# Another order in the opening of attention, weight loads behind the third row gather, and another chain at the list table

## Chip, cores and metric

One core of a Trainium2 chip runs the whole kernel. The metric is device time in microseconds of one launch; lower is better. The time before is the median of three runs.

## What is computed

Causal attention with a bias from a running sum, then a mixture of experts with greedy assignment by capacity, then a second mixture with top-1 routing and a residual:

```python
# attention: B=4, H=8, S=576, D=64, all float32
cum = np.cumsum(np.maximum(s, 0), -1)
scores = q @ k.T / 8 + np.minimum(-(cum[..., :, None] - cum[..., None, :]), 0)   # causal
attn = exp(scores - max) / (sum + 1e-9);  x = (attn @ v) as (2304, 512)
# first mixture: 8 experts, each takes 288 rows; the pairs (row, expert) in order of falling
# logit x @ w_gate; a row goes to the first expert that has room
for e: out[mask] = relu(x[mask] @ w1[e]) @ w2[e]
# second mixture: rows with x @ w_skip > 0 get x + prob * relu(x @ w1[e]) @ w2[e], e = argmax
```

## The kernel before, in words

PE's float32 products are made of two parts, a rounded high part (fp32r) and the low rest, so each product is two or three passes, and each operand has to be split first: a rounding copy (ACT or POOL) and a subtraction (DVE or POOL).

**Attention** works on 32 heads in groups of two (`G`), in steps `k`, three per head. Each step issues a hand-written order (`ORDER`) of scores (S, lines 236 and 237), masking (M, 248), exponentials (X, 256), transposes (T, 272), splits of the transposed weights (H, 286, and L, 291), the product with V (AV, 300) and the output. For a group `g`, `load_a` brings the raw rows of K and Q through SP (`load_raw`, line 80) and a rounded copy of them through POOL's DMA queue (line 88) into one of three buffers `KQ`. `load_b` puts four small DMAs with the running sums into the buffer (74, 75), copies halves of it into `ka` and `qa` by DMA on SP (140, 141), makes the low parts by POOL subtractions (143, 144; a pair for each of the two heads), and loads V (146). `vsplit` splits V on POOL (92, 93). Scores need `ka` and `qa`; AV needs the split V. Group 0 is split by DVE and ACT in `first_group`; the second head's low part is `low1` (110, 111). V of group 0 is split in `vload2`. `raw` has two buffers, so a load of raw rows waits for the subtractions of two groups before. Setup work for the later stages is interleaved on POOL through `gen`, one piece a step from step 9 on.

Every engine runs its queue in order. The sequence on POOL in the opening of the kernel before is: V split of group 0, subtractions of group 1, three memsets (387 to 389) that fill the constant rows of the third `KQ` buffer, the load of group 2, V split of group 1, the load of group 3, the subtractions of group 2.

**The first mixture.** `routing` finds for one expert at a time, by a search over the bit patterns on DVE with counts on PE, the logit threshold, and from it the 288 rows. They become three lists of 96 row numbers: a one-hot table `oh` (729) of each row's place, times the row's number in two digits `rv` (726), summed by 18 matmuls (734); two DVE operations (738, 739) turn the two digits into the row number `tok`. POOL gathers the rows by indirect DMA (993), PE transposes them (1004), ACT and DVE split them (1008, 1009). Then follow the first product with w1 (1018, 96 matmuls in eight blocks), and the second with w2 (1043, 1049). Weights come in eight loads of 512 KB for each expert: six are split by ACT (985) and DVE (987), two are used as they are. For the first expert SP issues loads 0 to 3, and ACT issues loads 4 to 7 (951) once it has converted the fourth. All this is not written in order by hand: each operation is given to a planner (`Plan`) with an engine, a cost, what it reads and writes, and a priority, and the planner's simulated start times set the order of every engine's queue, for the first mixture and the first expert of the second in one plan. `KN["nd"]` = 16 dummy matmuls (1410) are added after the lists, at the lowest priority. The table `oh` shares its tile with the constant `io1` (854, POOL).

Of the kernel before, what the change touches and what calls it, by code (L numbers as in the profile page):

```python
# [56 lines left out]
def attention(tc, ctx, consts, gen, kqT, kq0, vL, s, wgb, xs, logits, ident):  # L57
# [25 lines left out]
    def load_a(g):  # L83
        if g not in loads:
            load_raw(g)
        qb, kb, raw = QB[g % NQB], KB[g % NQB], loads[g]
        for sl in ((slice(0, 1), slice(1, 2)) if g == 1 else (slice(0, G),)):
            nc.gpsimd.dma_start(KQ[g % NQB][64:128, :, sl], kqT[g][:, :, sl])
        loads[g] = raw, qb, kb
# [41 lines left out]
    def load_b(g, eng, dq):  # L131
        h0 = g * G
        raw, qb, kb = loads.pop(g)
        qa = work.tile([128, G, S], F32R, name="qa")
        ka = work.tile([128, G, S], F32R, name="ka")
        vraw = work.tile([128, G, NB, D], F32, name="vraw", bufs=3)
        vhl = work.tile([128, G, NB, 2, D], F32R, name="vhl", bufs=3)
        aux_rows(h0, qb, kb)
        for sl in ((slice(0, 1), slice(1, 2)) if g == 1 else (slice(0, G),)):
            dq.dma_start(ka[0:64, sl].bitcast(F32), kb[64:128, sl].bitcast(F32))  # L140
            dq.dma_start(qa[64:128, sl].bitcast(F32), qb[64:128, sl].bitcast(F32))
        for i in range(G):
            eng.tensor_tensor(qa[0:64, i], raw[64:128, 1, i], qb[64:128, i].bitcast(F32), op=OP.subtract)  # L143
            eng.tensor_tensor(ka[64:128, i], raw[64:128, 0, i], kb[64:128, i].bitcast(F32), op=OP.subtract)
            if i == 0:
                nc.sync.dma_start(vraw, vL[g])
        grp[g] = (qa, ka, qb, kb, vhl, vraw)
        return lambda: vsplit(vraw, vhl, eng)
# [33 lines left out]
    nc.gpsimd.tensor_copy(gate, QB[0][0:4, G - 1, 0:1].bitcast(F32))  # L182
    load_a(1)
# [193 lines left out]
    if True:  # L377
        for k in range(nsteps + 12 + SK):
# [3 lines left out]
            if u0 and u0[1] == 1 and u0[0] % G == 0 and u0[0] // G + 1 < NH // G:  # L382
                g = u0[0] // G + 1
                if g == 1:
                    vload2()
                    fin = load_b(g, nc.gpsimd, nc.sync)
                    nc.gpsimd.memset(QB[2][0:64].bitcast(F32), 1.0)
                    nc.gpsimd.memset(KB[2][0:64].bitcast(F32), 0.0)
                    nc.gpsimd.memset(KB[2][0:4].bitcast(F32), 1.0)
                    load_a(g + 1)  # L390
                else:
                    if g + 1 < NH // G:
                        load_a(g + 1)
                    fin = load_b(g, nc.gpsimd, nc.sync)
                fin()
            if k == FILL:
                low1()
                fill()
# [132 lines left out]
def routing_consts(tc, consts, T):  # L531
# [16 lines left out]
    def steps():  # L548
# [8 lines left out]
        for o in range(2):  # L557
            v = c["vals"][64 * o:64 * o + 64]
            nc.gpsimd.iota(v[:, 0:4 * B, 0].rearrange("p (b n) -> p b n", b=B), pattern=[[S // 64, B], [2, 4]],
                           base=1 + o, channel_multiplier=0, allow_small_or_imprecise_dtypes=True)  # L560
            nc.gpsimd.iota(v[:, 4 * B:, 0], pattern=[[2 * S // 64, B // 2]], base=S // 64 * o, channel_multiplier=0,
# [23 lines left out]
def routing(tc, pool, P, c, lw, ph, ei_all, tok, rt, rb, T):  # L585
# [5 lines left out]
    sl_pr = -1 if ph == 0 else 1  # L591

# [113 lines left out]
    if not last:  # L706
        dve(0.08, "eo", "pn", lambda: V.tensor_scalar(pn, eo, -3e38, None, op0=OP.mult))
        dve(0.21, "pn", "lw", lambda: V.tensor_tensor(lw, lw, pn[:, None, :].to_broadcast(BC), op=OP.add))
        dve(0.08, "eo", "opn", lambda: V.tensor_tensor(opn, opn, eo, op=OP.subtract))
    dve(0.11, "pb", "inc", lambda: V.tensor_tensor_scan(inc, rt[:, 128:128 + 2 * NT], c["zero40"], 1.0, op0=OP.add,  # L710
# [4 lines left out]
    if not last:  # L715
        dve(0.08, "q", "q1", lambda: V.scalar_tensor_tensor(q1, q, CAP + 0.5, q, op0=OP.is_le, op1=OP.mult))
        dve(0.08, "q1", "nd", lambda: V.scalar_tensor_tensor(nd, q1, 0.5, nd, op0=OP.is_ge, op1=OP.add))

    rv, g4, p_, bk, iv = (T[n] for n in "rv g4 p_ bk iv".split())
# [12 lines left out]
    def lists():  # L732
# [5 lines left out]
    dve(0.075, "ib", "iv", lambda: V.tensor_copy(iv, rt[:96, 256:262].rearrange("p (k v) -> p k v", v=2)), sl_pr)  # L738
    dve(0.075, "iv", f"tok{ph}", lambda: V.scalar_tensor_tensor(  # L739
        tok[:, 3 * ph:3 * ph + 3], iv[:, :, 0], 64.0, iv[:, :, 1], op0=OP.mult, op1=OP.add), sl_pr)  # L740


def routing_tiles(pool):
# [26 lines left out]
    t("iv", [96, 3, 2])  # L770
# [59 lines left out]
def moe(tc, ctx, setup, lw, xs, w1, w2, w9, v1, v2, out, ident):  # L830
# [3 lines left out]
    for _ in gen:  # L834
# [20 lines left out]
                   allow_small_or_imprecise_dtypes=True)  # L855
    for i in (6, 7):
# [73 lines left out]
    def dmas():  # L930
        while done["dma"] < min(done["route"] * NCH, 2 * E * NCH):
# [5 lines left out]
            if p < E:  # L937
# [7 lines left out]
                if 4 <= n < 8:  # L945
                    if n == 4:
                        def ld(p=p):
                            reg["g"] = nc.scalar.value_load(ei_all[0:1, p:p + 1], min_val=0, max_val=E - 1)
                        op("ACT", 0.1, f"ei{p} wh3b", "regg", ld)
                    op("ACT", 0.07, "regg", key,  # L950
                       lambda p=p, dst=dst, k=k, src=src: nc.scalar.dma_start(
                           dst, src[ds(reg["g"], 1), k % 4].rearrange("o p f -> (o p) f")), xfer=1.456, lat=0.65)
# [14 lines left out]
    def conv():  # L967
# [19 lines left out]
        op("DVE", 1.13, f"raw{i} wh{j}a wh{j}b", v, lambda: V.tensor_tensor(  # L987
# [416 lines left out]

    def route(p):
        routing(tc, pool, cur["P"], rc, lw, p, ei_all, tok, rt, rb, T)
        done["route"] += 1
        if p == 0:
            for _ in range(KN["nd"]):
                op("PE", 0.43, "ib", "", lambda: nc.tensor.matmul(YB[0], rc["onesb"], T["ge"][:, 0:512], start=True,  # L1410
# [6 lines left out]
    for k in range(4):  # L1417
        conv()
    for k in range(3):
        xtr(0, k)  # L1420
    for p in range(E):
# [204 lines left out]
```

## Time and profile before

| | |
|---|---|
| median of three runs | 723.19 us (722.15 to 724.77) |
| the profiled execution | 724.78 us |
| its span in the trace | 723.1 us |
| PE busy, share of the span | 667.0 us, 92% |
| DVE busy | 531.7 us, 74% |
| ACT busy | 402.3 us, 56% |
| POOL busy | 269.2 us, 37% |
| mean granted PE clock | 0.960 |

The rows of the next sections come from this execution. In a timeline a row is: start in us, length in us, engine, line, operation, output<-inputs and sizes, xcount, and in brackets how long the engine had been idle and what released it. A queue of an engine (SPq, ACTq) shows DMA issues. The granted clock is a share of 2.4 GHz: 1.00 is that, 0.50 is 1.2 GHz. Attention takes the first 230 us, the first routing until 251, the first mixture until about 475, the second mixture the rest.

### The profile page before, as it was taken

What the parts mean: (1) busy time and instruction counts of PE and PEld (TensorE: products, weight loads), DVE (VectorE), ACT (ScalarE), POOL (GpSimd) and SP (SyncE); (2) the same over time, 40 slices, a digit from 0 to 9 for tenths busy, and PEclk for the clock granted to TensorE, in tenths of its full rate; (3) what the DMA queues carried; (4) which work ended last, traced back from release to release, by engine and by line L of the source; (5) the groups of instructions that cost most, each with busy time, mean ns of one, the idle gap of its engine ahead of it and who ended that gap; (6) DMA issues with size and microseconds to landing.
All of it is one profiled execution on the core that took longest, in us unless ns stands there. A gap on an engine that the chain in (4) does not pass through costs nothing. (4 is left out here: it accounts for less than half of the span.)

```text
span 723.1 us, 14104 instructions
## 1 busy us (share of the span) xinstructions
PE 667.0 (92%) x4667; PEld 581.1 (80%) x4667; DVE 531.7 (74%) x1604; ACT 402.3 (56%) x910; POOL 269.2 (37%) x379
## 2 busy tenths in 40 slices
PE   4789999999996469999999999999999999999996
PEld 4678989989895349787989898989988787777775
DVE  7668888898886656888888878763459449499544
ACT  8768888888883121443425242454347248487533
POOL 4899769968720420111112050522111321141201
PEclk9989999999998559999999989999999999999998
DMA  7868797797612340644527080943069219499320
GB/s 163 198 150 198 186 231 164 202 212 169 175 36 75 114 157 12 244 146 175 202 103 274 30 302 11 370 153 107 12 247 390 79 62 327 160 347 332 147 81 23
DMA packets 35939, 122.25 MB, mean 169 GB/s; under 512 B 6480, under 2 KB 6480, under 8 KB 34064
## 3 DMA queue, kind: packets, MB, share of 16 engines
q1 hardware_dynamic: 28272, 94.87, 41.2%
q0 software_dynamic: 7008, 24.25, 12.4%
q10 hardware_dynamic: 576, 2.10, 0.9%
q8 instruction: 43, 0.70, 0.4%
q14 instruction: 40, 0.33, 0.2%
HBM read 101.12 MB, written 13.76 MB: 159 GB/s over the span
## 5 line engine op out<-in xcount | busy, mean ns | idle before, releaser
L987 DVE TENSOR_TENSOR wl<-raw,wh 128x1024 fp32r<-128x1024 f32 x112 | 134.4, 1216 | 23.0 <-ACT wh L985 19.7
L985 ACT CAST wh<-raw 128x1024 fp32r<-128x1024 f32 x112 | 114.7, 1048 | 35.7 <-DMA raw<-in_w_dram 23.7
L256 ACT ACTIVATE z<-z,sums 128x576 f32<-128x576 f32 (+2 forms) x144 | 84.7, 589 | 3.2 <-DVE sums L248 1.6
L248 DVE CUSTOM_DVE_ANT_0 z<-s,mask 128x576 f32<-128x576 f32 (+2 forms) x144 | 70.3, 513 | 13.0 <-PE s L237 12.4
L272 PE MATMUL pt<-ident,z 128*128 128x128 f32 (+1 forms) x464 | 77.3, 282 | 1.1 <-DVE ptl L291 0.6
L993 POOL DMA_INDIRECT xb<-xs,k_tok x24 | 30.8, 1284 | 120.6 <-DVE k_tok L739 38.1
L291 DVE TENSOR_TENSOR ptl<-pt,pth 128x512 fp32r<-128x512 f32 (+2 forms) x128 | 68.0, 551 | 7.4 <-ACT pth L286 7.1
L236 PE MATMUL s<-kq 128*128 128x288 f32 (+2 forms) x192 | 63.8, 344 | 9.6 <-ACT kq L114 8.8
L1049 PE MATMUL y<-hf,rb 128*128 128x288 f32 x256 | 70.5, 411 | 0.0
L1093 POOL DMA_INDIRECT out_dram<-xb,k_tok x24 | 26.2, 1091 | 114.3 <-ACT xb L1076 97.8
L286 ACT CAST pth<-pt 128x512 fp32r<-128x512 f32 (+2 forms) x128 | 59.1, 473 | 10.9 <-PE pt L272 8.1
L237 PE MATMUL s<-ka,qa 128*128 128x288 f32 (+2 forms) x192 | 52.5, 309 | 7.5 <-DMA qa<-kq 4.6
L272 PEld LDWEIGHTS pt<-ident,z 128*128 128x128 f32 (+1 forms) x464 | 52.8, 142 | 6.2 <-issue 3.0
L1051 ACT CAST yr<-y 128x288 fp32r<-128x288 f32 x32 | 12.7, 398 | 74.1 <-PE y L1049 70.8
L1049 PEld LDWEIGHTS y<-hf,rb 128*128 128x128 f32 x256 | 45.5, 190 | 9.0
L1018 PE MATMUL h<-xth,wh 128*128 128x288 f32 x256 | 50.5, 318 | 2.0 <-DVE r_ac L663 0.9
L300 PE MATMUL y<-pth,vhl 128*128 128x384 f32 (+2 forms) x160 | 50.8, 326 | 0.2 <-ACT yT L317 0.2
L1018 PE MATMUL h<-xtl,wh 128*128 128x288 f32 x256 | 48.4, 309 | 0.1
L1018 PE MATMUL h<-xth,wl 128*128 128x288 f32 x256 | 48.1, 306 | 0.0
L236 PEld LDWEIGHTS s<-kq 128*128 128x128 f32 x192 | 37.0, 193 | 13.4 <-issue 11.1
L300 PE MATMUL y<-ptl,vhl 128*128 128x384 f32 (+2 forms) x160 | 46.6, 320 | 0.0
L143 POOL TENSOR_TENSOR qa<-raw,kq 64x576 fp32r<-64x576 f32 x30 | 42.6, 1419 | 4.3 <-DVE ptl L291 2.5
(343 smaller groups left out, 1736.5 us busy)
## 6 DMA issues: line engine op xcount, KB each, us to landing
raw<-in_v_dram SPq DMA_DIRECT2D x64, 512.0 KB
raw<-in_w_dram SPq DMA_DIRECT2D x46, 512.0 KB
raw<-in_kqT_dram SPq DMA_DIRECT2D x14, 576.0 KB
kq<-in_kqT_dram POOLq DMA_DIRECT2D x14, 576.0 KB
rb<-in_w_dram SPq DMA_DIRECT2D x14, 512.0 KB
vraw<-in_vL_dram SPq DMA_DIRECT2D x16, 320.0 KB
xs<-xb SPq DMA_DIRECT2D x16, 288.0 KB
ka<-kq SPq DMA_DIRECT2D x14, 288.0 KB
```

What stands on the lines that cost most here:

```text
L236: nc.tensor.matmul(rows[:, o + c0:o + c1], qs_, kb[:, i, c0:c1], start=True, stop=False)
L237: nc.tensor.matmul(rows[:, o + c0:o + c1], ql_, ka[:, i, c0:c1], start=False, stop=True)
L248: nc.vector.tensor_tensor_reduce(z[:, :w], ps[:, o:o + w], mk, op0=OP.add, op1=OP.min, scale=-0.125, scalar=3e38, accum_out=sums[h // 2][: ...
L256: nc.scalar.activation(z[:, :w], z[:, :w], AF.Exp, bias=sm[:, 0:1], scale=-1.0, accum_out=sm[:, 1:2])
L272: nc.tensor.transpose(ps[:jw, k, :], p[:, I0[jb]:I0[jb] + jw], ident)
L286: nc.scalar.copy(hview(PTB[h % 2][0], ib, jbs), ps[:, :len(jbs), :])
L291: nc.vector.tensor_tensor(hview(PTB[h % 2][1], ib, jbs), ps[:, :len(jbs), :], hview(PTB[h % 2][0], ib, jbs).bitcast(F32), op=OP.subtract)
L300: nc.tensor.matmul(y[:, a2 - 192:S - 192], vhl[:, h % G, jb].rearrange("p a d -> p (a d)"), PTB[h % 2][t][:, jb, a2 - 192:], start=n_ == 0 ...
L985: return nc.scalar.copy(WH[j], RAW[i])
L987: op("DVE", 1.13, f"raw{i} wh{j}a wh{j}b", v, lambda: V.tensor_tensor(WL[j], RAW[i], WH[j].bitcast(F32), op=OP.subtract), pr)
L1018: x = nc.tensor.matmul(ps, a[(p * HC + k) % NP][:, m * 128:(m + 1) * 128], xt[c][:, k, :], start=k == 0 and i == 0, stop=k == 3 and i == 2)
L1049: op("PE", 0.49, f"rb{r} hf{k}", f"yb{b}", lambda r=r, o=o, k=k: nc.tensor.matmul(ps, RB[r][:, o:o + 128], hf[:, k - HS1, :], start=False, ...
```

## The change

In the opening of attention, group 1 is loaded at step `FILL` (2), after `low1` and `fill`; POOL first does a small gate copy that reads what `low1` wrote, then the three memsets, then the subtractions of group 1's first head, V split of group 0, the load of group 2, and the second head's subtractions. The raw rows of the next group are issued on SP behind the group's own copies and V, in all groups. In the first routing, loads 4 to 7 are issued by SP behind a POOL copy that reads the third gathered tile; the fourth weight's subtraction stands behind the second tile's split. The table `oh` is first written by an ACT copy in the setup; the removal of the taken expert (`taken`) and two operations on `q1` and `nd` go behind the table; the row's number is stored as a multiple of 64 and a rest, so that one sum gives `tok`. The dummy matmuls read `oh` instead of `ge`.

```diff
     def load_a(g):
-        if g not in loads:
-            load_raw(g)
-        qb, kb, raw = QB[g % NQB], KB[g % NQB], loads[g]
         for sl in ((slice(0, 1), slice(1, 2)) if g == 1 else (slice(0, G),)):
             nc.gpsimd.dma_start(KQ[g % NQB][64:128, :, sl], kqT[g][:, :, sl])
-        loads[g] = raw, qb, kb
...
-    def load_b(g, eng, dq):
+    def load_b(g, eng, dq, mid=None):
         h0 = g * G
-        raw, qb, kb = loads.pop(g)
+        raw, qb, kb = loads.pop(g), QB[g % NQB], KB[g % NQB]
...
             if i == 0:
                 nc.sync.dma_start(vraw, vL[g])
+                if mid:
+                    mid()
...
+    load_raw(1)
     load_a(1)
...
                 g = u0[0] // G + 1
-                if g == 1:
-                    vload2()
-                    fin = load_b(g, nc.gpsimd, nc.sync)
-                    nc.gpsimd.memset(QB[2][0:64].bitcast(F32), 1.0)
-                    nc.gpsimd.memset(KB[2][0:64].bitcast(F32), 0.0)
-                    nc.gpsimd.memset(KB[2][0:4].bitcast(F32), 1.0)
-                    load_a(g + 1)
-                else:
-                    if g + 1 < NH // G:
+                if g > 1:
+                    more = g + 1 < NH // G
+                    if more:
                         load_a(g + 1)
                     fin = load_b(g, nc.gpsimd, nc.sync)
-                fin()
+                    if more:
+                        load_raw(g + 1)
+                    fin()
             if k == FILL:
                 low1()
+                nc.gpsimd.tensor_copy(gate, grp[0][0][0:4, 1, 0:1].bitcast(F32))
+                nc.gpsimd.memset(QB[2][0:64].bitcast(F32), 1.0)
+                nc.gpsimd.memset(KB[2][0:64].bitcast(F32), 0.0)
+                nc.gpsimd.memset(KB[2][0:4].bitcast(F32), 1.0)
+                load_b(1, nc.gpsimd, nc.sync, lambda: (vload2(), load_a(2), load_raw(2)))()
                 fill()
...
-            nc.gpsimd.iota(v[:, 0:4 * B, 0].rearrange("p (b n) -> p b n", b=B), pattern=[[S // 64, B], [2, 4]],
-                           base=1 + o, channel_multiplier=0, allow_small_or_imprecise_dtypes=True)
+            nc.gpsimd.iota(v[:, 0:4 * B, 0].rearrange("p (b n) -> p b n", b=B), pattern=[[S, B], [128, 4]],
+                           base=64 + 64 * o, channel_multiplier=0, allow_small_or_imprecise_dtypes=True)
...
+    sl_lw = 3 if ph == 0 else 0
...
-    if not last:
+    def taken(r=""):
-        dve(0.08, "eo", "pn", lambda: V.tensor_scalar(pn, eo, -3e38, None, op0=OP.mult))
+        dve(0.08, "eo" + r, "pn", lambda: V.tensor_scalar(pn, eo, -3e38, None, op0=OP.mult))
         dve(0.21, "pn", "lw", lambda: V.tensor_tensor(lw, lw, pn[:, None, :].to_broadcast(BC), op=OP.add))
         dve(0.08, "eo", "opn", lambda: V.tensor_tensor(opn, opn, eo, op=OP.subtract))
+    if not last and ph:
+        taken()
...
-        dve(0.08, "q", "q1", lambda: V.scalar_tensor_tensor(q1, q, CAP + 0.5, q, op0=OP.is_le, op1=OP.mult))
-        dve(0.08, "q1", "nd", lambda: V.scalar_tensor_tensor(nd, q1, 0.5, nd, op0=OP.is_ge, op1=OP.add))
+        dve(0.08, "q", "q1", lambda: V.scalar_tensor_tensor(q1, q, CAP + 0.5, q, op0=OP.is_le, op1=OP.mult), sl_lw)
+        dve(0.08, "q1", "nd", lambda: V.scalar_tensor_tensor(nd, q1, 0.5, nd, op0=OP.is_ge, op1=OP.add), sl_lw)
...
-    dve(0.075, "ib", "iv", lambda: V.tensor_copy(iv, rt[:96, 256:262].rearrange("p (k v) -> p k v", v=2)), sl_pr)
-    dve(0.075, "iv", f"tok{ph}", lambda: V.scalar_tensor_tensor(
-        tok[:, 3 * ph:3 * ph + 3], iv[:, :, 0], 64.0, iv[:, :, 1], op0=OP.mult, op1=OP.add), sl_pr)
+    if ph == 0:
+        taken(" oh")
+
+    def ids():
+        with nc.allow_low_precision(reason="whole numbers below 4096"):
+            return V.tensor_reduce(tok[:, 3 * ph:3 * ph + 3], rt[:96, 256:262].rearrange("p (k v) -> p k v", v=2),
+                                   axis=AX.X, op=OP.add)
+    dve(0.075, "ib", f"tok{ph}", ids, sl_pr)
...
+    nc.scalar.copy(T["oh"][:, :96], T["io1"])
...
                     if n == 4:
-                        def ld(p=p):
-                            reg["g"] = nc.scalar.value_load(ei_all[0:1, p:p + 1], min_val=0, max_val=E - 1)
-                        op("ACT", 0.1, f"ei{p} wh3b", "regg", ld)
-                    op("ACT", 0.07, "regg", key,
-                       lambda p=p, dst=dst, k=k, src=src: nc.scalar.dma_start(
-                           dst, src[ds(reg["g"], 1), k % 4].rearrange("o p f -> (o p) f")), xfer=1.456, lat=0.65)
+                        op("POOL", 0.1, "xr2", f"{key} dlg", lambda dst=dst: nc.gpsimd.tensor_copy(
+                            dst[0:1, 0:1], XB[2][0:1, 0:1]), 1)
+                    op("SP", 0.57, f"reg{p} dlg", key,
+                       lambda p=p, dst=dst, k=k, src=src: nc.sync.dma_start(
+                           dst, src[ds(reg[p], 1), k % 4].rearrange("o p f -> (o p) f")), xfer=1.456, lat=0.65)
...
-        op("DVE", 1.13, f"raw{i} wh{j}a wh{j}b", v, lambda: V.tensor_tensor(
+        op("DVE", 1.13, f"raw{i} wh{j}a wh{j}b" + (" xl1" if n == 3 else ""), v, lambda: V.tensor_tensor(
             WL[j], RAW[i], WH[j].bitcast(F32), op=OP.subtract), pr)
...
+    dm = T["oh"].rearrange("p a b -> p (a b)")[:, 0:512]
...
-                op("PE", 0.43, "ib", "", lambda: nc.tensor.matmul(YB[0], rc["onesb"], T["ge"][:, 0:512], start=True,
+                op("PE", 0.43, "ib", "", lambda: nc.tensor.matmul(YB[0], rc["onesb"], dm, start=True,
                                                                   stop=True), 5)
...
     route(0)
-    for k in range(4):
+    for k in range(3):
         conv()
-    for k in range(3):
+    for k in range(2):
         xtr(0, k)
+    conv()
+    xtr(0, 2)
```

## Rows read from the trace of the kernel before

**Rows 1.** The page, part 2: the granted clock of PE in 40 equal slices.

```profile
PEclk9989999999998559999999989999999999999998
```

**Rows 2.** Timeline of PE, opening of attention.

```profile
21.52 0.40 PE L237 MATMUL s<-ka,qa 128*128 128x288 f32 x1 [2.92 <-POOL ka L144]
...
22.05 0.42 PE L300 MATMUL y<-pth,vhl 128*128 128x384 f32 x1
...
28.42 0.38 PE L236 MATMUL s<-kq 128*128 128x288 f32 x1
...
34.09 0.38 PE L236 MATMUL s<-kq 128*128 128x288 f32 x1
...
39.04 0.58 PE L237 MATMUL s<-ka,qa 128*128 128x288 f32 x1 [4.58 <-DMA qa<-kq]
...
53.49 0.39 PE L236 MATMUL s<-kq 128*128 128x288 f32 x1
```

**Rows 3.** Windows: us, busy (x) of PE, PEld, DVE, ACT, POOL, PEclk, DMA share, GB/s.

```profile
24.00:26.00 2.00, 2.00 (x11) 1.75 (x10) 0.55 (x1) 1.06 (x2) 1.94 (x3) 0.50 0.33 51
...
40.00:42.00 2.00, 2.00 (x8) 2.00 (x7) 1.57 (x4) 0.82 (x3) 1.85 (x2) 0.50 0.83 207
```

**Rows 4.** Timeline of POOL, opening of attention.

```profile
16.17 0.72 POOL L92 CAST vhl<-vraw 128x640 fp32r<-128x640 f32 x1 [4.71 <-DMA vraw<-in_vL_dram]
...
18.61 1.40 POOL L143 TENSOR_TENSOR qa<-raw,kq 64x576 fp32r<-64x576 f32 x1
...
24.50 1.05 POOL L387 MEMSET kq<- 64x1152 f32 x1
...
27.61 0.56 POOL L88 DMA_DIRECT2D kq<-in_kqT_dram  x1
...
42.02 0.26 POOL L327 TENSOR_SCALAR rc<-sums 128x8 f32<-128x8 f32 x1
...
47.34 0.60 POOL L88 DMA_DIRECT2D kq<-in_kqT_dram  x1
```

**Rows 5.** Timelines of DVE and of SP's queue, opening of attention.

```profile
12.38 0.75 DVE L111 TENSOR_TENSOR qa<-raw,ql 64x576 fp32r<-64x576 f32 x1
...
33.32 0.51 SPq L140 DMA_DIRECT2D ka<-kq  x1
```

**Rows 6.** Timelines of POOL, ACT's queue and PE, gathers of the first two experts.

```profile
256.50 1.96 POOL L993 DMA_INDIRECT xb<-xs,k_tok  x1 [0.30 <-issue]
...
297.99 1.09 POOL L993 DMA_INDIRECT xb<-xs,k_tok  x1 [0.30 <-issue]
...
255.55 0.97 ACTq L951 DMA_DIRECT2D raw<-in_w_dram  x2
...
264.46 0.87 PE L1004 MATMUL tr<-ident,xb 96*128 96x96 f32 x4 [2.77 <-DMA xb<-xs,k_tok]
...
301.36 0.55 PE L1004 MATMUL tr<-ident,xb 96*128 96x96 f32 x4 [0.23 <-DMA xb<-xs,k_tok]
```

**Rows 7.** Windows around the first product of the first expert.

```profile
262.00:264.00 2.00, 0.00 (x0) 0.00 (x0) 0.20 (x2) 0.00 (x0) 0.00 (x0) 0.50 1.03 334
...
270.00:272.00 2.00, 2.00 (x10) 2.00 (x10) 1.52 (x3) 0.41 (x1) 0.00 (x0) 0.50 0.00 0
...
274.00:276.00 2.00, 2.00 (x17) 1.92 (x17) 0.81 (x3) 0.41 (x1) 0.00 (x0) 1.00 0.00 0
```

**Rows 8.** Timelines of DVE and ACT, first lists.

```profile
248.61 1.06 DVE L729 TENSOR_TENSOR oh<-r_p__76,oh 128x1728 bf16<-128x1728 bf16 x1 [0.59 <-DVE r_rv L726]
...
251.05 0.16 DVE L738 COPY r_iv<-rt 96x6 f32<-96x6 f32 x1 [1.29 <-PE rt L734]
...
250.08 1.05 ACT L985 CAST wh<-raw 128x1024 fp32r<-128x1024 f32 x1 [14.51 <-DMA raw<-in_w_dram]
```

**Rows 9.** Line 729: semaphore events on DVE's queue, ns min/median/max, first and last start.

```profile
L729 DVEq EVENT_SEMAPHORE  x9: 21/50/50, 247.8 to 248.5; - x9
```

**Rows 10.** Window over the change from the first to the second expert.

```profile
300.00:330.00 30.00, 28.27 (x256) 25.48 (x255) 24.98 (x95) 14.01 (x27) 3.47 (x8) 1.00 0.62 226
```

More of the change, by code (lines that the diff above doesn't have):

```diff
@@ L558, in steps @@
             v = c["vals"][64 * o:64 * o + 64]
-            nc.gpsimd.iota(v[:, 0:4 * B, 0].rearrange("p (b n) -> p b n", b=B), pattern=[[S // 64, B], [2, 4]],
-                           base=1 + o, channel_multiplier=0, allow_small_or_imprecise_dtypes=True)
-            nc.gpsimd.iota(v[:, 4 * B:, 0], pattern=[[2 * S // 64, B // 2]], base=S // 64 * o, channel_multiplier=0,
+            nc.gpsimd.iota(v[:, 0:4 * B, 0].rearrange("p (b n) -> p b n", b=B), pattern=[[S, B], [128, 4]],
+                           base=64 + 64 * o, channel_multiplier=0, allow_small_or_imprecise_dtypes=True)
+            nc.gpsimd.iota(v[:, 4 * B:, 0], pattern=[[2 * S, B // 2]], base=S * o, channel_multiplier=0,
                            allow_small_or_imprecise_dtypes=True)
@@ L715, in routing @@
     if not last:
-        dve(0.08, "q", "q1", lambda: V.scalar_tensor_tensor(q1, q, CAP + 0.5, q, op0=OP.is_le, op1=OP.mult))
-        dve(0.08, "q1", "nd", lambda: V.scalar_tensor_tensor(nd, q1, 0.5, nd, op0=OP.is_ge, op1=OP.add))
-    rv, g4, p_, bk, iv = (T[n] for n in "rv g4 p_ bk iv".split())
+        dve(0.08, "q", "q1", lambda: V.scalar_tensor_tensor(q1, q, CAP + 0.5, q, op0=OP.is_le, op1=OP.mult), sl_lw)
+        dve(0.08, "q1", "nd", lambda: V.scalar_tensor_tensor(nd, q1, 0.5, nd, op0=OP.is_ge, op1=OP.add), sl_lw)
+    rv, g4, p_, bk = (T[n] for n in "rv g4 p_ bk".split())
     oh = T["oh"]
@@ L769, in routing_tiles @@
     t("bk", [128, NT, 3])
-    t("iv", [96, 3, 2])
     t("lo2", [96, 24])
```

## The prediction

> **What bounds the kernel now.** I read the page's slices first, then windows of 2 us, then the timelines of PE, POOL and SP around the two places where the slices dip. The granted clock of PE (a slice is 18 us) is full from about 54 to 217 us and, but for one slice, from about 270 us on; it dips in the third slice and in slices 13 to 15 [rows 1]. It falls where PE idles, and where PE never idles a shorter wait elsewhere gives nothing: so I looked at the two dips alone.
>
> Dip one is the opening of attention. The first scores of head 2 wait 2.92 us for POOL's second subtraction (L144), those of head 4 wait 4.58 us for a copy into qa [rows 2]. After the second wait PE runs at 1.2 GHz: the granted clock is 0.50 at 40 to 42 us, as it is at 24 to 26 after the first [rows 3]. Undisturbed heads are 28.42 to 34.09 = 5.67 us apart; head 4 (34.09, first half) to head 6 (53.49) took 19.4 us for two heads [rows 2], 8 us too many. Behind both waits stands POOL's order [rows 4]: V split of group 0 at 16.17, four subtractions of group 1 from 18.61, three memsets from 24.50, and only at 27.61 the load of group 2. SP's copies of group 2 then leave at 33.32 [rows 5], 5.7 us later, and land at 39.04, another 5.7 us.
>
> Dip two is the first expert. The transposes of the third gathered tile wait 2.77 us and start at 264.46, 6.0 us after the gather was issued (256.50 plus 1.96); four weight loads were issued by ACT from 255.55 on [rows 6], and DMA is at share 1.03 while PE is idle [rows 7]. For the next expert the second gather's issue ended at 299.08 and PE had its tile at 301.36: 2.28 us [rows 6]. Here too the clock is down: 0.50 at 270 to 272 us with 10 matmuls, against 17 in 2 us at 1.00 [rows 7].
>
> **Opening, part by part.** POOL's jobs keep their number and length; their order changes. The new gate copy waits for low1, whose last operation ends at 12.38 + 0.75 = 13.13 [rows 5]. It costs about 0.3 (the nearest POOL operation of few elements is 0.26 at 42.02), then the memsets 24.50 to 27.61 = 3.1, a pair of subtractions (18.61 to 24.50, halved) 2.95, a V split (16.17 to 18.61) 2.44, a load 0.56 [rows 4]. So: memsets end at 16.6; POOL was waiting for V until 16.17, so they mostly fill idle time. Head 2's subtractions end at 19.5 (before, 21.5), V of group 0 at 22.0, group 2's load is issued by 22.6, the second pair ends at 25.5, V of group 1 at 27.9.
>
> The wait does not vanish: PE's weighted sum of head 0 stood at 22.05 [rows 2] and now waits for V until 22.0. I put the gain at head 2 at nothing, and the 2.0 us cover for head 2's scores is given back there. What gains is group 2: its load leaves at 22.0 instead of 27.61. With the same 5.7 us its copies leave at 27.7, and with the same 5.7 us they land at 33.4 instead of 39.04. POOL, free at 27.9, issues group 3's load and has head 4's subtractions done at 31.4, so the copy ends last, as before. Head 4 is wanted at 22.0 + (28.42 - 22.05) + 5.67 = 34.0, so its wait is gone and with it the cold stretch.
>
> Next late is head 6. POOL: group 2 done at 34.4, V split 36.8, the setup jobs (42.02 to 47.34, 5.3 us [rows 4]) 42.1, load and pair 45.7. PE wants it at 34.0 + 2 times 5.67 = 45.3. So head 6 starts at 45.7 instead of 53.49: 7.8 us. Bounds: 5.6 if only the load's lead survives, 3 if group 3's load and raw rows, which now run beside group 2's copies, slow these; I take **7.0**, near the POOL count because POOL ends last in it.
>
> The raw rows of the next group move on SP behind the group's copies and V. They are read only by the next group's subtractions; the copies stop waiting behind raw's buffer. PE is busy there, so 0; if that cover went, the copies' 5.7 us would show as a wait.
>
> **List table.** The one-hot table's write starts 0.59 us late [rows 8], behind nine semaphore events on DVE's queue [rows 9]. With ACT as last writer I expect one or two: 0.59 less, bounds 0 and 0.59. ACT's touching copy hides in the 14.51 us in which ACT waits for weights [rows 8]; uncovered it would delay the first weight by at most its length. One sum in place of copy and multiply-add takes one operation of 0.16 off the chain. The five operations moved behind the table fall into DVE's 1.29 us wait for the list matmuls [rows 8]: 0; without that cover they would hold up the row numbers by less than that wait. The new iotas have the old shapes: 0. Together **0.75**.
>
> **Weight gate.** The third gather's issue ends at 258.46 - 0.75 = 257.7; with 2.28 instead of 6.0 us it lands at 260.0, not 264.46: 4.5 us with the list's share, so **3.7** for the gate. Bounds: 0 if the gather is slow by itself, 4.7 if its issue also shrinks from 1.96 to the later 1.09 [rows 6]. The loads then start behind a POOL copy (0.26) and SP's in-order queue, where the second expert's loads stand behind them, whose expert is not known yet. Four 512 KB loads at 334 GB/s [rows 7] are 6.3 us: landed by about 268. The first product, 96 matmuls at 17 per 2 us, ends no earlier than 261 + 11.3 = 272.6. That is the cover; without it the second product waits. The Trainium skill (DMA: Bandwidth & Descriptors, Rules for kernel authors) says the opposite of this gate: issue a DMA early and wait on it late; by it these loads should stay where they are, and that case is the third rival. The fourth weight's subtraction goes behind the second tile's: its readers come eight matmuls after the last tile, so 0, and at most its own length. The dummy matmuls read another tile: 0.
>
> **Clock.** From 264.46 to 272 PE runs cold, 7.5 us; the same work at full clock would take 10/17 of it, 3.1 less. PE is idle throughout 262 to 264 us [rows 7]. With that stretch shorter the clock may rise sooner; bounds 0 and 3.1, I take **1.5**. The Trainium skill (TensorE: Matmul & The Clock Gate, HAM oscillation) says that waits between bursts throttle the engine anew each time; the trace agrees (0.50 at 262 to 264 us and at 40 to 42), and by it shortening a wait pays twice, or once if what is left still counts as idle.
>
> **Sum.** 7.0 + 0.75 + 3.7 + 1.5 = 13.0 us. The profiled execution took 724.78 us (span 723.1), 1.6 above the median of 723.19, so 711.8 on its own scale and **710.2** against the median.
>
> **Rivals.**
> 1. *The opening is bound by transfers.* Copies, V, raw rows and group 3's load share the engines; the attention term is 3, giving 714.2. For: both 5.7 us stretches. Against: DMA stood at share 0.33 at 24 to 26 us [rows 3], with the load not issued yet. Chance 0.15.
> 2. *The clock stays up* through the transposes: the clock term is 3.1 and the opening gives its 7.8, giving 707.8. Chance 0.13.
> 3. *Early issue was right*: the gather isn't helped, or the loads come back as a wait of the second product. The gate and clock terms vanish: 715.4. For: 2 MB move later. Against: 4.6 us of cover. Chance 0.10.
> 4. *It doesn't do what it says*: V replaces the scores as the wait, and nothing is issued earlier that counts; only the list's 0.75 is left, 722.4. Chance 0.05.
> 5. *Slower, by one mechanism:* the planner writes all eight experts' orders from its costs, and a new start gives a worse order. Each boundary between experts then idles PE more; it decides above 13.0 / 7 = 1.86 us each. At 2.5 us over seven boundaries it is +17.5, 727.7. Against: the worst stretch now has 1.73 us idle in 30 [rows 10]. Chance 0.03.
>
> **How the numbers follow.** The forecast has the remaining 0.54. The range takes in rivals 1, 2 and 3; below it adds the gather's bound (1.0) and the clock's and opening's overlap, 705.5; above, rival 3 with two of the four us that rival 1 takes, 717.5. About 0.3% (2.2 us) is what a measurement of this kernel can tell from no change: faster holds the forecast and rivals 1 to 3, 0.92; same is rival 4, 0.05; slower is rival 5, 0.03.
>
> **What would show it.** Right: POOL's memsets before its first subtraction and group 2's load near 22 us; no wait above 1 us at head 4's scores; clock 1.00 from 30 to 50 us; a one-hot write with few semaphore events; the third tile's transposes under 3 us behind the gather's issue, with no weight bytes before; the first product sooner at full clock. Wrong: head 4 still waiting over 3 us for qa, the third gather still 5 us under way, ACT stuck on the fifth weight inside the first product, or idle time growing at the experts' boundaries after 300 us.

## The result and the profile after

The changed kernel takes **713.43 us** (median of four runs, 712.41 to 713.93), the kernel before in the same session 723.36 (722.15 to 724.77): ratio 0.9854, 95% interval 0.9832 to 0.9877, some 10 us less. The profiled execution took 713.93 us, its span is 712.1, its mean granted clock 0.971. With the clock of [rows 1] that stood at 0.960 over 723.1, the clock that was not granted, (1 - clock) times the span, falls from 28.9 to 20.7 us.

The granted clock in the page's 40 slices, against [rows 1]:

```profile
PEclk9999999999998589999999999999999999999999
```

The first dip is gone in this view, the second is shorter. A stretch in which PE runs at 1.2 GHz is called cold below. Now the timeline of PE in the opening, against [rows 2]:

```profile
19.57 0.37 PE L236 MATMUL s<-ka,qa 128*128 128x288 f32 x1 [0.95 <-POOL ka L140]
...
21.94 0.44 PE L299 MATMUL y<-pth,vhl 128*128 128x384 f32 x1 [1.63 <-POOL vhl L89]
...
34.00 0.38 PE L235 MATMUL s<-kq 128*128 128x288 f32 x1
...
36.58 0.58 PE L236 MATMUL s<-ka,qa 128*128 128x288 f32 x1 [2.20 <-DMA qa<-kq]
...
50.52 0.39 PE L235 MATMUL s<-kq 128*128 128x288 f32 x1
```

Head 4 still waits for a copy into qa, 2.20 us instead of 4.58, and head 6 comes 2.97 us earlier (50.52 against 53.49). Behind it, the timelines of POOL and of SP's queue, against [rows 4, 5]:

```profile
16.59 1.42 POOL L139 TENSOR_TENSOR qa<-raw,kq 64x576 fp32r<-64x576 f32 x1
...
21.83 0.56 POOL L85 DMA_DIRECT2D kq<-in_kqT_dram  x1
...
30.01 1.42 POOL L139 TENSOR_TENSOR qa<-raw,kq 64x576 fp32r<-64x576 f32 x1 [1.80 <-DMA kq<-in_kqT_dram]
...
29.83 0.51 SPq L136 DMA_DIRECT2D ka<-kq  x1
```

POOL did what was forecast: its subtractions start at 16.59, group 2's load leaves at 21.83 (forecast 22.0). But SP's copies follow at 29.83, 8.0 us later and not 5.7, and PE has them at 36.58, 6.75 us after that. Windows of the same kernel (us, busy of PE, PEld, DVE, ACT and POOL, granted clock, DMA share, GB/s), against [rows 3, 7]:

```profile
24.00:26.00 2.00, 2.00 (x10) 1.75 (x10) 0.59 (x2) 1.06 (x2) 1.93 (x2) 0.50 1.12 214
...
38.00:40.00 2.00, 2.00 (x10) 2.00 (x8) 1.24 (x4) 0.70 (x3) 1.92 (x2) 0.54 0.97 219
40.00:42.00 2.00, 2.00 (x16) 1.53 (x16) 1.13 (x4) 1.61 (x4) 1.69 (x6) 1.00 1.04 225
...
258.00:260.00 2.00, 2.00 (x19) 1.85 (x18) 0.62 (x5) 0.00 (x0) 0.00 (x0) 0.57 0.92 295
260.00:262.00 2.00, 2.00 (x11) 1.85 (x11) 0.38 (x2) 1.31 (x2) 0.00 (x0) 0.58 0.99 377
...
320.00:322.00 2.00, 2.00 (x7) 1.57 (x7) 2.00 (x4) 1.05 (x1) 0.00 (x0) 0.50 1.02 418
```

DMA, at share 0.33 at 24 to 26 us before, is now full there, and the clock still falls. At the first expert it is low for 4 us (258 to 262), where before it was low from 262 to 272. It is low once more at 320 to 323 us, where before it was not, behind a wait of PE of 0.39 us. Last, DVE, POOL and PE at the first list and the first gathers, against [rows 6, 8, 9]; the second row groups the events of line 732:

```profile
244.74 1.06 DVE L732 TENSOR_TENSOR oh<-r_p__76,oh 128x1728 bf16<-128x1728 bf16 x1 [0.59 <-DVE r_rv L729]
...
L732 DVEq EVENT_SEMAPHORE  x9: 21/50/50, 243.9 to 244.6; - x9
...
252.09 1.96 POOL L1000 DMA_INDIRECT xb<-xs,k_tok  x1 [0.30 <-issue]
...
256.37 0.70 POOL L955 COPY raw<-xb 1x1 f32<-1x1 f32 x1 [2.33 <-DMA xb<-xs,k_tok]
...
256.45 0.52 PE L1011 MATMUL tr<-ident,xb 96*128 96x96 f32 x4 [0.80 <-DMA xb<-xs,k_tok]
...
257.54 1.69 PE L1025 MATMUL h<-xth,wh 128*128 128x288 f32 x8 [0.57 <-ACT xth L1015]
```

The table's write waits 0.59 us behind nine events exactly as before. The third tile is transposed at 256.45 instead of 264.46, 2.4 us after its gather's issue ended (252.09 + 1.96 = 254.05) and not 6.0.

**Where the 11 us come from**, by the start of the same instruction in the two profiled executions: first compare of the first routing -3.75 (231.45 to 227.70), third transposes -8.01, second expert's first output -10.52 (326.92 to 316.40), third expert's -8.01, fifth expert's -11.57 (440.21 to 428.64), last matmul -11.07 (716.51 to 705.44). (The first mixture runs to about 550 us in the kernel before, not to 475: the last of its outputs is rounded at 549.11.) So attention gives 3.75, list and gate 4.3 more, and the rest moves up and down among the later experts, a part that the prediction had not priced.

### The profile page after: what moved, and what is told of

Read it like the earlier page. It is cut to its first block, busy times and chain, and to the rows that moved or that the text cites. A ratio compares the mean times of both kernels' runs of the same rounds, so it can differ in the third digit from the quotient of the medians.

```text
span 712.1 us, 14096 instructions
## 1 busy us (share of the span) xinstructions
PE 661.9 (93%) x4666; PEld 576.3 (81%) x4667; DVE 531.1 (75%) x1596; ACT 404.0 (57%) x911; POOL 270.9 (38%) x381
## 5 line engine op out<-in xcount | busy, mean ns | idle before, releaser
L1100 POOL DMA_INDIRECT out_dram<-xb,k_tok x24 | 23.5, 980 | 137.4 <-ACT xb L1083 128.9
L1056 PE MATMUL y<-hf,rb 128*128 128x288 f32 x256 | 72.4, 417 | 0.0
L1000 POOL DMA_INDIRECT xb<-xs,k_tok x24 | 35.7, 1486 | 86.1 <-issue 50.3
L1025 PE MATMUL h<-xth,wh 128*128 128x288 f32 x256 | 48.5, 310 | 1.7 <-DVE hhl L1038 0.9
L235 PEld LDWEIGHTS s<-kq 128*128 128x128 f32 x192 | 37.0, 193 | 13.5 <-issue 11.3
L1025 PE MATMUL h<-xtl,wh 128*128 128x288 f32 x256 | 46.7, 303 | 0.0
L1025 PE MATMUL h<-xth,wl 128*128 128x288 f32 x256 | 46.5, 301 | 0.0
```

The lines of the kernel that those rows point to most:

```text
L235: nc.tensor.matmul(rows[:, o + c0:o + c1], qs_, kb[:, i, c0:c1], start=True, stop=False)
L1025: x = nc.tensor.matmul(ps, a[(p * HC + k) % NP][:, m * 128:(m + 1) * 128], xt[c][:, k, :], start=k == 0 and i == 0, stop=k == 3 and i == 2)
L1056: op("PE", 0.49, f"rb{r} hf{k}", f"yb{b}", lambda r=r, o=o, k=k: nc.tensor.matmul(ps, RB[r][:, o:o + 128], hf[:, k - HS1, :], start=False, ...
```

## The experiments

Each ratio is against the kernel before, run beside it on the same chip; the medians of before differ from session to session (723.4 to 727.6), so ratios are compared. Starts within a profile differ by 1 us and more between executions of the same code: the first compare of the first routing stands at 231.45 to 232.79 us in the four kernels with the opening of before, and at 227.25 to 228.72 in the seven with the opening of the changed kernel. By the means of these the opening is worth 3.8 us.

| kernel | median us | ratio, 95% interval |
|---|---|---|
| opening alone | 723.47 | 0.9935 (0.9899 to 0.9970) |
| gate alone | 726.88 | 0.9992 (0.9968 to 1.0015) |
| list alone | 723.55 | 0.9948 (0.9928 to 0.9968) |
| list alone, other price for the planner | 720.80 | 0.9964 (0.9943 to 0.9985) |
| opening and list, no gate edit | 717.78 | 0.9896 (0.9857 to 0.9936) |
| changed, loads ungated | 714.20 | 0.9873 (0.9841 to 0.9906) |
| changed, touch by DVE, second level | 714.40 | 0.9824 (0.9790 to 0.9858) |
| changed, touch by DVE, fifth level | 714.77 | 0.9840 (0.9798 to 0.9882) |
| changed, old dummy tile | 711.50 | 0.9841 (0.9810 to 0.9871) |
| changed, group 3's load later | 711.13 | 0.9807 (0.9767 to 0.9846) |
| changed, group 2's load earlier | 709.67 | 0.9787 (0.9747 to 0.9827) |
| changed, earlier load and touch | 710.83 | 0.9834 (0.9803 to 0.9864) |

**1. The opening alone.** The kernel before with the edits of `load_a`, `load_b` and the attention loop:

```diff
...
+load_b(1, nc.gpsimd, nc.sync, lambda: (vload2(), load_a(2), load_raw(2)))()
...
```

> The kernel before with the attention opening of the change alone; the experts' orders stay those of before. Theory (opening bound by transfers: the copies of group 2 land later than the prediction took them): heads 4 to 7 come 2.5 to 3.0 us earlier, PE still waits about 2 us for qa at head 4, time about 720.3 us. Rival (the prediction's own opening term of 7.0): no wait above 1 us at head 4, time about 716.3. Rival (POOL's memsets and subtractions alone moved, nothing that counts): 723.3.

Measured 0.9935, some 4.7 us; the interval, 2.2 to 7.3, takes in the expected 3 and the 7 of the prediction, so the trace has to decide. The written order of PE's matmuls is that of before. The first routing starts 3.07 us earlier. PE's timeline at head 4:

```profile
36.87 0.58 PE L236 MATMUL s<-ka,qa 128*128 128x288 f32 x1 [4.03 <-DMA qa<-kq]
```

The wait was not the 2 us expected: PE came to head 4 at 32.84 (36.87 - 4.03) in this run, whose clock did not fall at 24 us, 1.5 us ahead of the changed kernel (36.58 - 2.20 = 34.38), and waited until 36.87, nearly the same time. The landing sets head 4's time, whatever PE does before it. In all seven kernels with this opening PE waits there, 2.20 to 4.03 us. From the issue of group 2's load to head 4's scores it is 14.0 to 15.2 us in these seven, and 11.2 to 11.5 in the four with the opening of before. How the sum divides is less steady: 6.6 to 8.4 us for the load and 5.6 to 8.6 for the copies.

**2. The gate alone.**

```diff
+op("POOL", 0.1, "xr2", f"{key} dlg", lambda dst=dst: nc.gpsimd.tensor_copy(
+    dst[0:1, 0:1], XB[2][0:1, 0:1]), 1)
...
-nc.scalar.dma_start(
+nc.sync.dma_start(
...
```

> The kernel before with the weight gate alone (POOL copy, the four loads on SP, the third tile's transposes behind the fourth weight). Theory (the gate frees the third gather and PE keeps what it gains): transposes of the third tile at 260.5 instead of 264.5, first product about 4.5 earlier, time about 718.6 us. Rival (the planner's new order of the later experts adds to it, as the drift from -9 to -11 us between expert 1 and the end suggests): about 716.5. Rival (early issue was right, the loads come back as a wait of a later product): 722 to 723.5.

Measured 0.9992, no change. The third transposes start at 262.18, although its first routing began 1.34 us later than before: 3.6 us gained at the place forecast. PE at the second expert's transposes:

```profile
302.94 0.83 PE L1003 MATMUL tr<-ident,xb 96*128 96x96 f32 x4 [1.83 <-DMA xb<-xs,k_tok]
```

And a window right behind it:

```profile
304.00:306.00 2.00, 2.00 (x12) 1.85 (x12) 1.23 (x5) 0.95 (x4) 0.00 (x0) 0.50 1.03 383
```

PE arrives earlier and waits 1.83 us for the second expert's third gather, whose issue came only 1.1 us earlier (298.30 against 299.39), then runs at 1.2 GHz. Of 3.6 us only 1.1 is left at the third list, and by the last output none. The expected 718.6 fell, and with it the idea that each term is kept.

**3. The list alone**, with the touch, the one sum, the moved operations and the dummies' tile:

```diff
+nc.scalar.copy(T["oh"][:, :96], T["io1"])
...
-dve(0.075, "ib", "iv", ...
+dve(0.075, "ib", f"tok{ph}", ids, sl_pr)
...
```

> The kernel before with the list edits alone (ACT's touch, one sum, five operations behind the table, dummy matmuls on another tile). Theory (ACT's touch doesn't help, since the table's write still waits on all DMA semaphores): 0.59 us of wait and nine semaphore events ahead of the table's write as before, row numbers 0.2 to 0.4 earlier, time 722.9. Prediction's term of 0.75: one or two events, time 722.5. The two are told apart by the trace, not by the time. Rival (the planner's later orders change with it): more than 1.5 us from the time of before either way.

Measured 0.9948, some 3.8 us: much more than the 0.35 us that the list itself gained (first compare +0.63 against before, row numbers +0.28). PE at the third tile, and then a window in the fifth expert:

```profile
265.96 0.87 PE L1012 MATMUL tr<-ident,xb 96*128 96x96 f32 x4 [5.56 <-DMA xb<-xs,k_tok]
```

```profile
424.00:426.00 2.00, 2.00 (x24) 1.93 (x21) 1.89 (x8) 2.00 (x4) 0.26 (x3) 1.00 0.97 313
```

Without the gate nothing is gained here: the third gather is issued when it was before (256.45 against 256.50 us) and the tile comes 1.5 us later; PE, there sooner, waits 5.56 us. The gain is elsewhere. In the kernel before, PE's row ahead of the same place and the windows there:

```profile
422.78 0.85 PE L1018 MATMUL h<-xth,wh 128*128 128x288 f32 x2 [0.92 <-DVE r_ac L663]
```

```profile
424.00:426.00 2.00, 2.00 (x10) 2.00 (x10) 2.00 (x3) 0.00 (x0) 1.91 (x1) 0.50 0.97 369
426.00:428.00 2.00, 2.00 (x18) 1.85 (x17) 0.27 (x1) 1.34 (x2) 1.70 (x2) 0.50 1.04 418
```

Before, a 0.92 us wait on a routing step is followed by a cold stretch in the fifth expert, 10 matmuls in 2 us; with the list edits the planner writes another order of PE's matmuls, that wait is not there, and the clock stays at 1.00. The first output of the fifth expert is 2.15 us earlier, though the routing was 0.63 late and the fourth expert's first output 0.42 late. The stretch is in the opening-alone and gate-alone profiles too, whose orders there are those of before, and in no profile with the list edits.

That the wait as such makes the stretch is not shown. The list edits bring a longer one at another place, and the clock stays up there; PE in the same run, and the window around it:

```profile
402.55 0.17 PE L1146 MATMUL rb<-q_sel,onesb 96*128 96x24 bf16 x1 [1.04 <-DVE r_ge L625]
```

```profile
402.00:404.00 2.00, 1.45 (x19) 1.37 (x19) 1.76 (x4) 0.00 (x0) 0.00 (x0) 1.00 0.24 80
```

Ten of the eleven profiles with the list edits have such a wait, of 1.04 or 1.05 us, and the clock falls behind it in none.

**4. The same instructions in another order.** The list kernel with one number changed, the price that the planner sees:

```diff
-dve(0.075, "ib", f"tok{ph}", ids, sl_pr)
+dve(0.28, "ib", f"tok{ph}", ids, sl_pr)
```

> The list edits alone on the kernel before, as in the earlier run, but with the one sum priced for the planner like the two operations that it replaces (0.28 instead of 0.075 us). Every instruction is the same; only the written order of the experts' work changes. Theory (the list edits gained by a new order, which took a 0.92 us wait and its cold stretch out of the fifth expert): another order gives another time, 1.5 us or more from the list edits alone, and the cold stretch at 424 to 430 us is there or not with it. Rival (the gain is the shorter chain in each expert): within 0.7 us of the list edits alone.

Measured 0.9964 against 0.9948: by the ratios not to be told apart, so the expected 1.5 us did not show in the runs. In the profiles it is 2.4 us less than the list kernel (last output 713.42 against 715.85), and the fifth expert is warm in both:

```profile
424.00:426.00 2.00, 2.00 (x24) 1.93 (x23) 2.00 (x3) 0.58 (x2) 2.00 (x1) 1.00 1.03 412
```

What this settles is little: two new orders both lose the cold stretch. In this one 3.1 us are gained between the first compare and the fourth expert's first output, where the list kernel gained 0.2, and 1.9 more in the fifth expert: so the cold stretch is not the whole gain. That the shorter chain in each expert has no part in it is not shown.

**5. The touch by DVE itself, twice.**

```diff
-nc.scalar.copy(T["oh"][:, :96], T["io1"])
...
+if ph == 0 and lv == 1:   # then: lv == mid
+    dve(0.06, "geb", "oh", lambda: V.memset(T["oh"][0:1, 0:1, 0:1], 0.0))
```

> The changed kernel with the table's memory touched by DVE itself (one element, in the second level of the first routing, where DVE waits for PE's counts) in place of ACT's copy. Theory (the events belong to the engine that touches first, so only DVE's own earlier touch takes them off): nine events move to the touch, the table's write waits 0.1 us or less, row numbers 0.4 to 0.6 earlier than in the changed kernel, time about 712.9. Rival (the events move, but their 0.5 us now delays the levels instead): routing's end unchanged, 713.4.

> The changed kernel with DVE's own touch of the table three levels later than in the run before it, in the fifth level of the first routing, where DVE waits 0.50 us for PE's counts and the last rows of attention have landed. Theory (the earlier touch failed only because it met a row still under way, 1.39 us of wait): no DMA wait at the touch, levels at most 0.1 us longer, table's write with no event ahead of it, row numbers 0.5 us earlier measured from the first level; total about 0.5 us under the changed kernel's. Rival: the nine events do not fit into the 0.50 us and the levels grow by what the table gains, total unchanged.

In the second level the touch met a row of attention still on its way to memory; DVE's timeline:

```profile
230.81 0.06 DVE L628 MEMSET oh<- 1x1 bf16 x1 [1.39 <-DMA xs<-xb]
```

The levels end 0.98 us later, the list gains 0.68 of it back. In the fifth level it costs almost nothing; DVE's timeline, and the events of the touch:

```profile
235.84 0.06 DVE L628 MEMSET oh<- 1x1 bf16 x1 [0.28 <-issue]
...
L628 DVEq EVENT_SEMAPHORE  x8: 21/50/50, 235.1 to 235.7; - x8
...
245.07 1.05 DVE L734 TENSOR_TENSOR oh<-r_p__76,oh 128x1728 bf16<-128x1728 bf16 x1
```

The events went to the touch and the table's write has no wait: from first compare to row numbers 18.78 us (228.72 to 247.50) against 19.47 in the changed kernel, 0.69 less. So the events belong to the first access of each engine, and ACT's copy does not help DVE. In the compiled program the changed kernel's write still waits on sixteen DMA semaphores, with the touch on none. The totals (0.9824, 0.9840) are not told apart from the changed kernel's.

**6. Group 2 and 3's loads.** Group 3's load behind group 2's subtractions:

```diff
-if more:
+if more and g > 2:
     load_a(g + 1)
 fin = load_b(g, nc.gpsimd, nc.sync)
+if more and g == 2:
+    load_a(g + 1)
```

> The changed kernel with the POOL load of group 3 moved from ahead of group 2's subtractions to behind them, so that it no longer runs beside group 2's copies (ka, qa). Theory (group 3's load slows the copies: 6.75 us from issue instead of 5.7): copies land 1 us or more earlier, the wait of head 4 falls from 2.20 to 1.2 us or less, and 1 us of the total goes unless head 6 then waits. Rival (the copies are slow by themselves): wait of head 4 2.0 to 2.4 us, total unchanged or later by what group 3 loses.

Group 2's load ahead of the V split of group 0:

```diff
-lambda: (vload2(), load_a(2), load_raw(2))
+lambda: (load_a(2), vload2(), load_raw(2))
```

> The changed kernel with the POOL load of group 2 issued ahead of the V split of group 0 (19.5 us instead of 21.8). Theory (issue time is what counts, as the prediction took it): the load lands 2.3 us earlier, the wait of head 4 falls from 2.20 to under 0.5 us, V comes 0.6 us later, total 1 to 1.5 us less. Rival (the bytes of raw rows, V and this load under way together set the landing): the load takes longer from its issue, 9 us or more instead of 8.0, the wait of head 4 stays above 1.5 us, total within 0.7 us of the changed kernel's.

With group 3's load later, PE at head 4:

```profile
33.97 0.37 PE L236 MATMUL s<-ka,qa 128*128 128x288 f32 x1 [1.06 <-DMA qa<-kq]
```

The copies were issued at 29.18 and land 4.8 us later, less than in any of the seven kernels with group 3's load beside them (5.6 to 8.6): it had slowed them. The first routing starts 2.38 us before that of the changed kernel; by the ratio, 0.9807, the two are not told apart. With group 2's load earlier, POOL, SP and PE:

```profile
19.98 0.56 POOL L85 DMA_DIRECT2D kq<-in_kqT_dram  x1
...
25.96 0.51 SPq L136 DMA_DIRECT2D ka<-kq  x1
...
35.04 0.38 PE L235 MATMUL s<-kq 128*128 128x288 f32 x1
...
35.26 0.29 PE L236 MATMUL s<-ka,qa 128*128 128x288 f32 x1
...
47.63 0.39 PE L235 MATMUL s<-kq 128*128 128x288 f32 x1
```

The load leaves 1.9 us earlier and its copies 3.9 us earlier: it takes 6.0 us and not 8.0 (6.6 to 8.4 in the seven), now ahead of the raw rows of its group (20.27 us) instead of behind them. Head 4 waits for nothing, the clock is 1.00 from 28 us on, the first routing starts 2.87 us before that of the changed kernel, and the last output 3.84. Ratio 0.9787, its interval just clear of the changed kernel's (not run in the same session); **709.67 us is the lowest median of all kernels here.**

**7. The gate in its place.** The changed kernel with ACT's loads of before, and with loads on SP that wait for nothing:

```diff
...
-op("SP", 0.57, f"reg{p} dlg", key,
+op("SP", 0.57, f"reg{p}", key,
```

> The changed kernel without the weight gate: the opening and the list edits stay, ACT issues the four loads as in the kernel before. Gate alone gave next to nothing, since the second expert's third gather then waited 1.83 us. Theory (with the list edits the second expert's gathers come early enough, and the gate's gain is kept): about 3 us over the changed kernel. Rival (the gate is worth as little here): within 1 us of it, and the whole gain is opening plus list.

> The changed kernel without the POOL copy that gates the four loads: SP issues them as soon as the expert is known, right behind the first four, with nothing waiting for the gathers. Theory of the prediction (the gathers lose to 2 MB of weights): the third tile's transposes come 2 to 4 us later than in the changed kernel, total 2 to 3.5 us over it. Third rival (issue early): the loads are largely through before the gathers are issued, transposes within 1 us of the changed kernel's and no later wait, total the same or less.

PE with ACT's loads, then PE with ungated loads, and a window of the latter inside the first product:

```profile
261.13 0.87 PE L1012 MATMUL tr<-ident,xb 96*128 96x96 f32 x4 [2.92 <-DMA xb<-xs,k_tok]
```

```profile
260.32 0.88 PE L1008 MATMUL tr<-ident,xb 96*128 96x96 f32 x4 [0.34 <-DVE xtl L1013]
```

```profile
264.00:266.00 2.00, 2.00 (x10) 2.00 (x9) 1.27 (x1) 0.00 (x0) 0.00 (x0) 0.50 0.00 0
```

Against ACT's loads the gate is worth 4.7 us at the third tile and 3.7 at the last output, of which 1.0 was lost in attention already: 2.8 for the gate. By the profiles it is kept beside the list edits, and alone it was not; the intervals of the ratios (0.9896 and 0.9854) overlap. Against the ungated loads it is worth 3.9 us at the third tile and 4.2 at the first product, and nothing some 95 us later: the third expert's first output is at 355.99 against 356.13, the last output 1.1 later; by the ratios (0.9873, 0.9854) the two are not told apart. The second expert's number, behind which SP loads its weights, is not held up by the late product: 276.25 against 277.37 us. The planner's order of the later experts changes with this edit, so the 1.1 us are not the gate's alone. What the total owes to the gate itself, and not to taking the loads off ACT, is not shown.

**8. The dummies' tile, and the best pieces together.**

```diff
-nc.tensor.matmul(YB[0], rc["onesb"], dm, start=True
+nc.tensor.matmul(YB[0], rc["onesb"], T["ge"][:, 0:512], start=True
```

> The changed kernel with the dummy matmuls on the tile of before (ge, which the next routing writes) instead of the list table. The prediction priced this edit at 0. Theory now (ge makes them wait 1.43 us for DVE in the kernel before, and the clock there rises at 258 instead of 252 us): a wait of about 1.4 us inside the dummies, PE at 0.50 up to the transposes, and 262 to 270 us cold again as with the gate alone (0.57); first product up to 3 us later at its end, total 1 to 2.5 us over the changed kernel. Prediction: no difference.

PE at the dummies, and a window in the first product, both with the old tile:

```profile
251.27 1.87 PE L1417 MATMUL y<-r_ge,onesb 128*128 128x512 bf16 x4 [1.43 <-DVE r_ge L623]
```

```profile
260.00:262.00 2.00, 2.00 (x23) 1.86 (x23) 1.16 (x2) 1.36 (x2) 0.00 (x0) 1.00 1.01 401
```

The wait of 1.43 us came as expected, the rest was wrong: PE stays at 2.4 GHz through the first product, and from its start to the second expert's number it is 18.47 us instead of 19.83. The clock rose later, between 254 and 256 us instead of 250 and 252, and did not fall. Total 0.9841, not told apart from the changed kernel's. The edit's price of 0 is not refuted.

> The changed kernel with the two pieces that helped: group 2's load ahead of the V split of group 0, and DVE's own touch of the table in the fifth level. Theory (they touch separate places): the attention 2.9 us earlier, the list 0.6 us shorter, total about 4.4 us under the changed kernel, near 709. Rival (the 0.6 us of the list is lost behind the gathers): the same as with the earlier load alone, 3.8 us under.

Measured 710.83, 0.9834: the earlier load's gain is there (first compare -3.10), the list's 0.68 too (row numbers -3.78), and at the first product the clock is down again, 8 matmuls in the window; by the last output -2.6 is left. That is less than the 3.8 of the rival, and by the ratio it is not told apart from the changed kernel: the touch is not worth adding here. The window:

```profile
254.00:256.00 2.00, 1.91 (x8) 1.91 (x8) 0.56 (x1) 0.04 (x1) 0.00 (x0) 0.50 0.74 227
```

## Why the prediction was right, and where it was not

The total held: 710.2 forecast, 713.43 measured, inside 705.5 to 717.5. Its sum of 13.0 stands against 9.9 by the medians and 10.85 by the profiled executions. That the time lies inside the range is luck in part: the opening gave some 3 us less than its term, and a gain without a term, from another written order of the experts' work, made up for most of it.

- **Opening, 7.0: mis-sized, 3.8 by the means of eleven profiles.** The step that failed is "with the same 5.7 us its copies leave at 27.7, and with the same 5.7 us they land at 33.4". Head 4 was wanted when forecast (34.38 against 34.0 us), but the load took 8.0 us and the copies 6.75, together 14.75 and not 11.4, since raw rows and group 3's load ran beside them. That is the first rival in mechanism and price; its counter-argument, DMA at share 0.33, held only while the load wasn't issued. Experiment 6 shows both parts: ahead of the raw rows the load takes 6.0 us, without group 3's load the copies 4.8. The "0" for the raw rows' move looked at SP's order and not at the load that stands behind them. Of the prediction's own signs, the 2.20 us at head 4 lie between the 1 us named for right and the 3 us named for wrong; in the other six kernels with this opening it is 2.29 to 4.03.
- **Head 6: wanted too early.** The spacing of 5.67 us was read between heads 3 and 4. With no wait and the clock at 1.00 heads 4 to 6 take 12.59 us (35.04 to 47.63, experiment 6) and not 11.34, so of the "8 us too many" some 1.2 were work, and with head 4 at 34.0 head 6 comes at 46.6: 6.9 us and not 7.8 at the most.
- **List, 0.75: mis-sized, 0.33.** "With ACT as last writer I expect one or two" events: nine remained, 0.59 us with them. What was gained is the one operation less and its gap (0.21 between the table's write and the row numbers) and 0.12 ahead of the write. Experiment 5 shows why the events stayed.
- **List, what it moves: not foreseen.** The term counted the first expert alone. By experiment 3 the list edits give some 3.8 us (0.9948), most of it in the fifth expert, where another written order goes without a wait of 0.92 us and the cold stretch behind it; in the second order of experiment 4 more than half comes ahead of that. The prediction had a new order only as the rival that makes it slower; here it made the kernel faster.
- **Gate, 3.7: right at its place.** The third tile gained 3.9 beyond the list's share, 2.4 us behind its gather's issue where 2.28 was forecast. What the term left out is the next expert: alone, the gain became a 1.83 us wait there. By the profiles it is kept with the list edits beside it; loads on SP without the gate end at a total that is not told apart (experiment 7). The cover was 4.3 us and not 4.6: 261 + 11.3 is 272.3.
- **Early issue, the third rival.** The Trainium skill (DMA: Bandwidth & Descriptors, Rules for kernel authors) says to issue a DMA early and to wait on it late. At the place itself the trace disagrees, 3.9 us later at the third tile; over the whole kernel it neither agrees nor disagrees, 0.9873 against 0.9854.
- **Clock, 1.5: half of it, and partly by luck.** From third transposes (-8.01) to the write of the second expert's number (-8.77) 0.8 us were gained. But whether the first product runs cold changes from one nearly equal kernel to the next: low at 258 to 262 us in the changed kernel, not with the old dummies or the earlier load, low at 254 with the touch. From its start to that number it is 18.47 and 19.12 us in the two kernels with gated loads where it stays at 1.00 and 19.10 to 20.11 in the five where it falls, so the term should have been a range and no value. Nor are the 0.8 us the clock's alone: with ungated loads the number comes 14.48 us behind the start of a product that is cold. The Trainium skill (TensorE: Matmul & The Clock Gate, HAM oscillation) says that waits between bursts throttle the engine anew, by which a shorter wait can pay twice. At head 4 the traces agree in part: with 4.58 us of wait the clock is below 0.70 from 36 to 44 us, with 2.20 from 36 to 40, and with 1.06 or none (experiment 6) not at all; but with 4.03 (experiment 1) it is low no longer than with 2.20.

What stays open: how much of the list's gain is order and how much the shorter chain of the later experts, what of the total is the gate's, and what decides whether the clock falls, at the first product and behind a short wait.

## What to carry to other kernels

Price a transfer that is moved forward by what will then be on the engines beside it, not by its duration at the old place; put the one that somebody waits for ahead of those that nobody does. A gain at one gather or wait is only kept if the next stage's input moves with it, so a term is not finished at the place where it arises. Where a planner orders the work, an edit of 0.2 us can change the order and the cold stretches far away: 6.8 us at 1.2 GHz were gone from the fifth expert here. Look for such stretches in the trace first, and do not price them by the wait ahead of them alone.

## What was not expected of the hardware

- A wait on semaphores has a price of its own even when all have long been signalled: nine events of 21 to 50 ns, 0.59 us on DVE, and another engine's earlier access to the same memory does not take them away.
- DMA at a share of 0.97 to 1.12 moves very different amounts: 214 to 225 GB/s in the opening, 313 to 418 GB/s in the experts (the windows above).
- The granted clock can be low while PE is busy throughout: 2.00 of 2.00 us in both windows at 258 to 262 us in the changed kernel, at 0.57 and 0.58, with the last waits (0.80 and 0.57 us) before 257.6; and at 320 to 322 us at 0.50, behind a wait of 0.39 us. Behind waits of 1.04 us it stayed at 1.00 (experiment 3).
